# A fused attention and gated-FFN kernel: w_down loaded ahead of the x turns, the last FF-tile pair in 7 products, wo apart from down for token pair 0

## The chip, the cores and the metric

The kernel runs on one core of a Trainium2 chip. The metric is the device time of one execution, in microseconds (us). A core has a matrix engine (TensorE, PE in the profile), a vector engine (VectorE, DVE), a scalar engine (ScalarE, ACT), a general one (GpSimd, POOL) and SyncE (SP), which here only issues transfers. The engines run side by side and wait for each other by semaphores.

## The reference, cut to what matters

x has 2048 tokens of 512 features. It is normalized to xn. An attention branch A and a gated branch B both read xn, and their outputs are added to x:

```python
xn  = layernorm(x)                                       # 2048 x 512
q, k, v = split(xn @ wqkv)                               # 32 heads of 16
phi = lambda t: concat(softmax(t @ w_phi), softmax(-(t @ w_phi)))
kv  = sum_s phi(k)[s]^T v[s];  z = sum_s phi(k)[s]        # per head
o   = (phi(q) @ kv) / (phi(q) @ z + 1e-6)
A   = o @ wo
B   = ((xn @ w_gate) * (xn @ w_up)) @ w_down             # F = 1792
out = x + A + B
```

## The kernel before, in words

**Tiles.** The tokens are 16 tiles of 128 (t), 4 groups of 512 (sg), and 8 pairs of tiles (p) for the output. F is 14 FF tiles of 128 (ft); tiles ft and ft+7 form a pair, so there are 7 FF-tile pairs.

**Gate and up.** `U(ft, sg)` computes gate and up of one FF tile for one group: 4 + 4 matmuls of 512 columns, an eviction of gate by ACT (`ge`), and a multiplication on DVE that reads up from PSUM and writes `hT` (`h`). `BLOCK(kind, ft, ..)` does the same for an FF-tile pair and groups 1 and 2 at once, by a 2 x 2 scheme with 7 products in place of 8 (`b1` to `b7`, each 2 matmuls of 512 columns). It needs sums of weights (`WSUMS`, 4 on POOL for each block, `gw`, `uw`), sums of xn (`XSUMS`, 8 on DVE, `Xs`), and more evictions: seeds and copies on ACT (`sd`, `s7`, `s2`), adds on DVE (`a4`, `a5`). `NB` says how many pairs are done so. Group 3 is done later in halves of 256 tokens (`U2`, steps `gu`).

**Attention.** `K(t)`, `V(t)` and `KV(t)` build kv tile by tile; the features need a sum on DVE (`kr`), a reciprocal on ACT (`kc`) and two operations on POOL (`kq`, `kp`). `KVX` copies kv out. `Q(t)` makes the features of q (`qq`, `qp` on POOL) and turns them by a DMA (`qT`). `NUM(t)` multiplies by kv, divides, and turns the result by a DMA (`oT`).

**Down and wo.** Down is also a 2 x 2 scheme over each token pair, with 7 products `P1` to `P7` of 7 matmuls of 256 columns, sums of w_down (`TSUMS`, `Ts`, 16 on POOL) and of h (`SSUMS`, `S`, 4 on POOL for each pair). wo is joined in one of two ways. `CAT_STEPS(p)` puts wo into the same 7 products (2 more matmuls each, `P1o` to `P7o`), with 4 POOL sums of o for each pair (`SOSUMS`, `So`). `DOWN_STEPS(p)` adds wo in full to three products and one further group (`W22`), with no sums of o. `CAT` lists the pairs that take the first way.

**Normalization.** `LN(ts)` takes statistics on DVE (`st`, `ag`), scales on ACT into a ring of 4 slots (`nm`), and turns the tile by a DMA on SP (`xT`). So nm8 can be written only after xT4 has read its slot.

**Order.** Nothing runs in the order of the code. Each operation is recorded as a step with the regions that it reads and writes. A planner (`_plan`) then places the steps on each engine by costs, priorities and readiness, and the instructions are emitted in that order, with the semaphores that they need. `sc.chain` fixes the order of some steps: SP's loads and turns are one such chain. `PACE` and `SL` spread the block units over the K/V loop, and `UE`, `QP0`, `QP1` place group 3 and Q within the output pairs. Line 1449 holds w_down's place:

```python
sc.chain("x12 xT4 xT5 xT6 xT7 xT8 xT9 xT10 xT11 wd xT12 xT13 wT0 wo xT14 xT15")
```

Most instructions carry the line of a helper: L524 every matmul, L477 the evictions on ACT, L795 every sum (POOL, and DVE for XSUMS), L745 and L743 `kp`/`qp` and `kq`/`qq`, L825 and L876 the products h, L882 the adds of a block, L736 `kr`, L1203 the adds of down.

Of the kernel before, what the change touches and what calls it, by code (L numbers as in the profile page):

```python
# [57 lines left out]

class _Step:
    __slots__ = ("eng", "fn", "idx", "deps", "sig", "lane", "semval", "known", "waits", "is_out", "cost", "lat",  # L60
                 "prio", "seq", "start", "finish", "kind", "name", "nbytes", "ns", "win", "order", "lock", "reserve")

    def __init__(self, eng, fn, idx, lane):
        self.eng = eng
        self.fn = fn
        self.idx = idx
        self.deps = []
        self.sig = False
        self.lane = lane
        self.semval = None  # L70
        self.known = {}
        self.waits = []
        self.is_out = False
        self.cost = 100.0
        self.lat = 180.0
        self.prio = 0
        self.seq = 0
        self.start = 0.0
        self.finish = 0.0
        self.kind = ""  # L80
        self.name = ""
        self.nbytes = 0
        self.ns = ()
        self.win = 60.0
        self.order = []
        self.lock = False
        self.reserve = 0.0


# [111 lines left out]
def _plan(sc):  # L201
    nsteps = len(sc.steps)
    remaining = [0] * nsteps
    dependents = [[] for _ in range(nsteps)]
    for st in sc.steps:
        uniq = {id(d): d for d in st.deps}
        st.deps = list(uniq.values())
        remaining[st.idx] = len(st.deps)
        for d in st.deps:
            dependents[d.idx].append(st)  # L210
        for d in st.order:
            if id(d) not in uniq:
                remaining[st.idx] += 1
                dependents[d.idx].append(st)
    ready = {e: [] for e in sc.by_eng}
    ready_time = [0.0] * nsteps
    T0 = {PE: 800.0, ACT: 800.0, DVE: 800.0, POOL: 800.0, SP: 800.0}
    for st in sc.steps:
        ready_time[st.idx] = T0[st.eng]
        if remaining[st.idx] == 0:  # L220
            ready[st.eng].append(st)
    free_at = dict(T0)
    new_order = {e: [] for e in sc.by_eng}
    global_order = []
    dma_free = 0.0
    scheduled = 0
    while scheduled < nsteps:
        best = None
        for e in sc.by_eng:
            lst = ready[e]  # L230
            if not lst:
                continue
            fa = free_at[e]
            s0 = min(max(ready_time[st.idx], fa) for st in lst)
            cand = min((st for st in lst if max(ready_time[st.idx], fa) <= s0 + st.win),
                       key=lambda st: (st.prio, st.idx))
            s = max(ready_time[cand.idx], fa)
            if cand.lock:
                s = max(s, free_at[POOL])
            if best is None or s < best[0]:  # L240
                best = (s, cand)
        if best is None:
            raise RuntimeError("scheduling deadlock")
        start, st = best
        e = st.eng
        ready[e].remove(st)
        st.start = start
        if isinstance(st.lane, tuple):
            free_at[e] = start + st.cost
            if st.kind == "turn":  # L250
                d0 = max(start + st.cost + 410.0, dma_free)
                st.finish = d0 + st.nbytes / 182.0 + st.reserve
                dma_free = d0 + st.nbytes / 182.0 * 0.5
            else:
                d0 = max(start + st.cost + 1500.0, dma_free)
                dma_free = d0 + st.nbytes / 305.0
                st.finish = dma_free + (2500.0 if st.nbytes > 300000 else 0.0)
        else:
            free_at[e] = start + st.cost
            st.finish = free_at[e] + st.lat + st.reserve  # L260
            if st.lock:
                free_at[POOL] = max(free_at[POOL], free_at[e])
        st.seq = len(new_order[e])
        new_order[e].append(st)
        global_order.append(st)
        scheduled += 1
        for dep_st in dependents[st.idx]:
            remaining[dep_st.idx] -= 1
            in_order = st.eng == dep_st.eng and (st.eng == PE or not any(d is st for d in dep_st.deps))
            ready_time[dep_st.idx] = max(ready_time[dep_st.idx], free_at[e] if in_order else st.finish)  # L270
            if remaining[dep_st.idx] == 0:
                ready[dep_st.eng].append(dep_st)
    sc.by_eng = new_order
    sc.est_finish = max(st.finish for st in sc.steps)
    return global_order
# [76 lines left out]

XENG = DVE
LN12 = 6
FT = 7
QAT = [11, 12, 13, 14]
NB = 6
RS = 1
PA = -1
PD = -1  # L360
# [5 lines left out]
AB = {7: (2, 3)}  # L366
CO = {}
CH = "P6.7 P2.7 P5.7 P4.7 P3.7"
NX = 0
ZP = 0  # L370
WSE = POOL
# [2 lines left out]
NRA = ()  # L374
SD = ()
SPL = ((0, 7),)
UE = 1.6
QP0 = 1
QP1 = 2
QA = 4  # L380
PQ = -1
TRQ = 1500.0
TRO = 800.0
PS = -1
CAT = (0, 1, 2, 3, 4, 5, 6)
SOE = POOL
TOE = POOL
PLN = 0
RX = 1500.0
RG = 0.0  # L390
NSW = 2


SL = 11.5


def PACE(t, n):
# [3 lines left out]
def _build(nc, es, A_x, A_wqkv, A_w_phi, A_wo, B_w_gate, B_w_up, B_w_down, out):  # L401
# [68 lines left out]
    sc = _Sched(nc)  # L470
# [323 lines left out]
    def sums(eng, out_, a_, b_, op, name, prio=None):  # L794
        fn = lambda e: e.tensor_tensor(out=out_, in0=a_, in1=b_, op=op)  # L795
        n = out_.free_size()
        if eng == POOL:
            pool(fn, parts(a_) + parts(b_), parts(out_), 100.0 + 2.0 * n, name=name, prio=prio or 0)
        else:
            st = dve(fn, parts(a_) + parts(b_), parts(out_), cost=60.0 + 0.53 * n, name=name, prio=PX if prio is None else prio)  # L800
            st.lock = True
            st.reserve = RX if prio is None else 0.0

    hT_v = sbv("hT", 0, NF * 1536).bitcast(F16).rearrange("p (f s) -> p f s", f=NF)
# [596 lines left out]
    NA3 = len(units)  # L1401
    units += [(U2, ft, 1792) for ft in std]
    ui = [0]

    def weight(u):
        return 4 if u[0] is U2 or u[0] is U else 0 if u[0] is ZWSUMS else 1

    def nextU():
        if ui[0] < len(units):
            u = units[ui[0]]  # L1410
            if ui[0] == n0:
                ring_banks[0] = [2, 3, 4, 5]
            u[0](*u[1:])
            ui[0] += 1

# [8 lines left out]
    LN([8, 9], prio=PLN)  # L1424
    LN([10, 11], prio=PLN)
    load_wT(0)
    kvn = [0]

    def KVS(t, lag):
        while kvn[0] <= t - lag:  # L1430
            KV(kvn[0])
            kvn[0] += 1
    for t in range(NT):
# [10 lines left out]
        KVS(t, 3 if t < QAT[0] - 3 else 2)  # L1444
        if t == FT:
            FOLD(0)
    sc.dma(SP, wd_v, B_w_down.rearrange("(f p) j -> p f j", p=128), 1835008, writes=[wd_v], name="wd")
    load_sq(SP, wo_v, A_wo.rearrange("(q p) j -> p q j", p=128), 524288, "wo")
    sc.chain("x12 xT4 xT5 xT6 xT7 xT8 xT9 xT10 xT11 wd xT12 xT13 wT0 wo xT14 xT15")
    TSUMS()  # L1450
    V(NT - 1)
    KVS(NT, 2)
    SSUMS(0)
    assert ui[0] >= NA
    load_x(SP, 4, 4, name="rx")
    load_x(SP, 8, 4, name="rx")
    down = CAT_STEPS(0) if 0 in CAT else DOWN_STEPS(0)
    nextU()
    KVS(NT, 1)
    KVX()  # L1460
    ring_banks[0] = [0, 1, 2, 3]
    rp[0] = 0
    nextU()
    if 0 not in CAT:
        down[0]()
        down[1]()
    NUM(0)
    nextU()
    if 0 not in CAT:
        SSUMS(1)  # L1470
    nextU()
    NUM(1)
    TOSUMS(TOE)
    if 0 in CAT:
# [6 lines left out]
        cum.append(cum[-1] + weight(u))  # L1481
    u0 = ui[0]
    NP = NT // 2
    for p in range(NP):
        def some(fr):
            k = cum[-1] * min(1.0, (p + fr) / (NP - UE))
            while ui[0] < len(units) and cum[ui[0] - u0] + weight(units[ui[0]]) / 2 <= k:
                nextU()
        if p == ZP and NX:
            ZXSUMS()  # L1490
            for b_ in blocks[:3]:
                ZWSUMS(*b_)
        a, b = 2 * p + 2, 2 * p + QA
        if p == 2:
            load_x(SP, 12, 4, name="rx", slot=0)
        def Qs(pos):
            for k, at in ((0, QP0), (1, QP1)):
                if at == pos and b + k < NT:
                    Q(b + k)
        if p in AB:  # L1500
            ring_banks[0] = [0, 1]
        if p > 0:
            down = CAT_STEPS(p) if p in CAT else DOWN_STEPS(p)
            Qs(0)
            down[0]()
            some(0.1)
            Qs(1)
            down[1]()
        some(0.2)
        if a < NT:  # L1510
            NUM(a)
        if p == 0:
            Qs(0)
            Qs(1)
        Qs(2)
        down[2]()
        some(0.4)
        Qs(3)
        down[3]()
        if 2 <= p + 1 < NP and p + 1 not in SLATE:  # L1520
# [12 lines left out]
        some(1.0)  # L1533
        if p + 1 in SLATE:
            SSUMS(p + 1)
        down[7]()
# [46 lines left out]
```

The softmax here doesn't subtract the row's maximum and nothing guards it: scores larger than these inputs give would overflow.

## Time and profile before

| | |
|---|---|
| time, median of 4 runs | 211.43 us (210.92 to 211.73) |
| time of the profiled execution | 210.92 us |
| its span, first to last instruction | 209.1 us |
| granted TensorE clock | 1.0 |
| busy: PE, POOL, DVE, ACT | 204.9, 174.1, 158.5, 113.7 us |
| loads of x, 512 KB: issue to landing (median) | 5.3 us |
| load of w_down, 1792 KB: issue to landing | 7.8 us |

Times in rows of the profile are us from the start of the span. Busy time of PE is modelled at its ends, so a full PE is not PE at its peak. "PEld" is the load of weights into PE ahead of matmuls. In rows of groups the numbers behind the bar are the busy time in us, the mean of one in ns, and the idle time of the engine before them with what ended it. In rows of a time line they are the start and the length in us.

### The profile page before, as it was taken

The page shows a single profiled execution, that of the slowest core. Times are in us where ns is not written, and L with a number is a line of the kernel's source. Part 1 is how long each engine was busy: PE and PEld are TensorE (multiplying, and loading weights), DVE is VectorE, ACT ScalarE, POOL GpSimd, SP SyncE. Part 2 cuts the span into 40 slices and gives each one's busy share as a digit, 9 for nine tenths or more (in the row PEclk, how much of TensorE's full clock was granted, in tenths as well). Part 3 has the DMA queues.
Part 4 walks back from the last instruction along what each step waited for, and adds up shares of the span by engine and source line. Part 5 has one row for each costly group of instructions (what it writes and reads, how often), then busy time and mean ns, then how long its engine had stood idle before and what let it go on. Part 6 is the DMA issues. An engine that isn't in the chain of part 4 may idle for free.

```text
span 209.1 us, 4281 instructions
## 1 busy us (share of the span) xinstructions
PE 204.9 (98%) x1616; PEld 135.7 (65%) x1616; DVE 158.5 (76%) x305; ACT 113.7 (54%) x293; POOL 174.1 (83%) x223
## 2 busy tenths in 40 slices
PE   8999999999999999999999999999999999999995
PEld 3875444444454444444446797888879888789884
DVE  4857799998966797989988766848659486584753
ACT  4756999698796959697822633315244151431000
POOL 4071698439999999999999999999999999997640
PEclk9999999999999999999999999999999999999999
DMA  5999724965100000223621217455351655435121
GB/s 173 330 277 371 211 61 97 342 115 144 37 16 0 3 0 0 50 52 53 193 60 28 50 25 138 91 128 105 70 131 25 141 38 115 91 75 129 27 75 50
DMA packets 50244, 21.52 MB, mean 103 GB/s; under 512 B 37424, under 2 KB 50224, under 8 KB 50224
## 3 DMA queue, kind: packets, MB, share of 16 engines
q1 hardware_dynamic: 49552, 20.93, 41.3%
q10 hardware_dynamic: 672, 0.33, 0.6%
q8 instruction: 12, 0.20, 0.4%
q14 instruction: 8, 0.07, 0.1%
HBM read 10.24 MB, written 2.10 MB: 59 GB/s over the span
## 4 chain that ended last, share of the span: by engine, by line
PE 81%; ACT 7%; POOL 4%; DVE 3%; DMA 3%; issue 1%; DVEq 0%
PE ps L524 79%; ACT arena L477 7%; DMA arena<-arena 3%; PE ps L1345 2%; POOL arena L795 2%; POOL arena L745 1%; DVE arena L641 1%; DVE arena L795 1%; DVE arena L736 1%; DVE arena L825 0%; POOL arena L743 0%; ACT ps L477 0%; DVE arena L643 0%; DVE arena L1203 0%; POOL arena L650 0%
## 5 line engine op out<-in xcount | busy, mean ns | idle before, releaser
L524 PE MATMUL ps<-arena 128*128 128x256 bf16 (+5 forms) x1606 | 200.7, 287 | 0.9 <-ACT ps L477 0.3
L524 PEld LDWEIGHTS ps<-arena 128*128 128x128 bf16 (+1 forms) x1606 | 134.4, 98 | 67.8 <-ACT arena L477 2.0
L795 POOL TENSOR_TENSOR arena<-arena 128x256 f16<-128x256 bf16 (+3 forms) x128 | 129.3, 1032 | 7.4 <-DMA arena<-arena 3.4
L477 ACT ACTIVATE arena<-ps 128x512 bf16<-128x512 f32 (+3 forms) x168 | 83.1, 533 | 65.2 <-PE ps L524 62.1
L736 DVE TENSOR_REDUCE arena<-arena 128x64 f32<-128x1024 bf16 x32 | 38.7, 1211 | 0.9 <-ACT arena L477 0.9
L1203 DVE TENSOR_TENSOR arena<-ps,arena 128x256 bf16<-128x256 f32 (+1 forms) x56 | 23.1, 421 | 17.9 <-PE ps L524 16.3
L477 ACT ACTIVATE arena<-arena 128x64 f32<-128x64 f32 (+4 forms) x96 | 28.4, 314 | 13.7 <-DVE arena L736 10.4
L745 POOL TENSOR_TENSOR arena<-arena 128x512 bf16<-128x512 bf16 x32 | 33.7, 1056 | 0.2
L1069 DVE TENSOR_TENSOR arena<-ps,arena 128x256 f16<-128x256 f32 x30 | 12.6, 421 | 11.1 <-ACT arena L477 11.0
L876 DVE TENSOR_TENSOR arena<-ps,arena 128x512 f16<-128x512 f32 x24 | 16.1, 684 | 1.0 <-PE ps L524 0.8
L825 DVE TENSOR_TENSOR arena<-ps,arena 128x512 f16<-128x512 f32 x14 | 9.5, 687 | 4.1 <-PE ps L524 2.5
L770 DVE TENSOR_TENSOR arena<-ps,arena 128x512 bf16<-128x512 f32 x16 | 10.9, 684 | 2.1 <-ACT arena L477 1.5
L641 DVE BATCH_NORM_STATS2 arena<-arena 128x6 f32<-128x512 bf16 x16 | 10.5, 675 | 1.9 <-DMA arena<-in_A_x_dram 1.9
L882 DVE TENSOR_TENSOR ps<-ps,arena 128x512 f32<-128x512 f32 x12 | 8.2, 696 | 4.3 <-PE ps L524 3.0
L1137 DVE TENSOR_TENSOR arena<-ps,arena 128x512 bf16<-128x512 f32 x16 | 11.0, 686 | 0.3
L743 POOL TENSOR_TENSOR arena<-arena 128x32 f32<-128x32 f32 x32 | 8.2, 260 | 3.2 <-ACT arena L477 3.2
L650 POOL TENSOR_SCALAR arena<-arena 128x1 f32<-128x1 f32 x12 | 3.3, 288 | 6.9 <-ACT arena L477 6.9
L623 POOL TENSOR_TENSOR arena<-arena 128x128 bf16<-128x128 bf16 x4 | 1.6, 425 | 8.5 <-DMA arena<-in_A_w_phi_dram 8.5
L882 DVE TENSOR_TENSOR arena<-ps,arena 128x512 bf16<-128x512 f32 x12 | 8.0, 680 | 0.0
L477 ACT ACTIVATE ps<-ps 128x512 f32<-128x512 f32 x12 | 7.2, 600 | 0.0
L1133 DVE RECIPROCAL arena<-arena 128x32 f32<-128x32 f32 x16 | 5.6, 352 | 0.5
L1345 PE MATMUL ps<-const-bfloat16-1.0 128*128 128x512 bf16 x10 | 4.4, 623 | 0.8 <-PEq L1568 0.8
(22 smaller groups left out, 26.0 us busy)
## 6 DMA issues: line engine op xcount, KB each, us to landing
arena<-in_A_x_dram SPq DMA_DIRECT2D x6, 512.0 KB, 5.3
arena<-in_B_w_down_dram SPq DMA_DIRECT2D x1, 1792.0 KB, 7.8
out_dram<-arena SPq DMA_DIRECT2D x14, 128.0 KB, 2.0
arena<-in_B_w_gate_dram SPq DMA_DIRECT2D x1, 768.0 KB, 7.2
arena<-in_B_w_up_dram SPq DMA_DIRECT2D x1, 768.0 KB, 8.8
arena<-arena SPq DMA_TRANSPOSE x44, 2.5
arena<-in_B_w_gate_dram SPq DMA_DIRECT2D x2, 256.0 KB, 4.2
arena<-in_B_w_gate_dram SPq DMA_DIRECT2D x1, 512.0 KB, 5.9
```

The costliest lines, as they stand in the source:

```text
L477: return e.activation(out=out_ap, in_=in_ap, func=func, scale=scale, **kw)
L524: ins = e.matmul(o, lhsT=l, rhs=r, start=s, stop=p, skip_group_check=True)
L641: dve(lambda e, t=t: e.bn_stats(stats_v[:, t, :], x_tile(t)), [x_tile(t)], [stats_v[:, t, :]], cost=600.0, name=f"st{t}", win=win, prio=prio)
L736: dve(lambda e, ei=ei, so=so: e.tensor_reduce(out=so, in_=ei.rearrange("p (h f) -> p h f", f=16), axis=AX.X, op=ALU.add), [ei], [so], cost ...
L745: pool(lambda e: e.tensor_tensor(out=ev[:, :, 1, :], in0=ev[:, :, 1, :], in1=ratio[:, :, None].to_broadcast([128, H, 16]), op=ALU.mult), [ ...
L770: dve(lambda e: e.tensor_tensor(out=o1, in0=src, in1=rp_[:, :, :, None].to_broadcast([128, 8, 4, 16]), op=ALU.mult), [src, rs_v[:, t % 4, ...
L795: fn = lambda e: e.tensor_tensor(out=out_, in0=a_, in1=b_, op=op)
L876: dve(lambda e: e.tensor_tensor(out=h, in0=src, in1=g, op=ALU.mult), [src, g], [h], name=f"h{ft}.{sg}", prio=PD)
L882: dve(lambda e: e.tensor_tensor(out=o, in0=src, in1=sn, op=ALU.add), [src, sn], [o], name=name, prio=PD)
L1069: dve(lambda e: e.tensor_tensor(out=h, in0=bank(b, 256 - GLO, 256), in1=g, op=ALU.mult), [bank(b, 256 - GLO, 256), g], [h], name=f"h{ft}.{ ...
L1137: dve(lambda e: e.tensor_tensor(out=ov, in0=src, in1=wv4[:, :, :, None].to_broadcast([128, 8, 4, 16]), op=ALU.mult), [src, w], [o], cost=6 ...
L1203: dve(lambda e: e.tensor_tensor(out=out_, in0=in_ps, in1=in_sb, op=ALU.add), [in_ps, in_sb], [out_], cost=328.0, name=f"{name}.{p}")
```

## The change

Three things and the settings that go with them. w_down's load stands after x12 in SP's chain, ahead of all turns of x (`WDP`), and its step is recorded earlier. `NB` is 7, so gate and up of all seven pairs take the 7 products in groups 1 and 2, and the four units `U` of tiles 6 and 13 there are gone. `CAT` begins at 1: pair 0 takes `DOWN_STEPS`. Group 3's units are not issued ahead of the pair loop any more (`nextT`, `p_done`). `FT`, `UE`, `QP1`, `SL` and `RX` have new values. The planner also gets a rule for DVE sums that are marked `sync`, which makes a POOL step wait for them.

```diff
-                 "prio", "seq", "start", "finish", "kind", "name", "nbytes", "ns", "win", "order", "lock", "reserve")
+                 "prio", "seq", "start", "finish", "kind", "name", "nbytes", "ns", "win", "order", "lock", "sync", "slip", "reserve")
...
             if st.lock:
                 free_at[POOL] = max(free_at[POOL], free_at[e])
+                if st.sync:
+                    port.append([st, st.slip, st.slip > 1])
+            elif e == POOL:
+                for q in port:
+                    if q[2] and last_pool is not None and last_pool not in st.deps:
+                        st.deps.append(last_pool)
+                    q[2] = False
+                    q[1] -= 1
+                    if q[1] <= 0 and q[0] not in st.deps:
+                        st.deps.append(q[0])
+                port = [q for q in port if q[1] > 0]
...
-FT = 7
+FT = 8
-NB = 6
+NB = 7
+WDP = 'x12'
+TT = None
...
-UE = 1.6
+UE = 1.8
-QP1 = 2
+QP1 = 3
...
-CAT = (0, 1, 2, 3, 4, 5, 6)
+CAT = (1,2,3,4,5,6)
...
-RX = 1500.0
+RX = 0.0
...
-SL = 11.5
+SL = 11.85
...
             st.lock = True
+            st.sync = prio is not None
+            st.slip = SLIP
             st.reserve = RX if prio is None else 0.0
...
     load_wT(0)
+    sc.dma(SP, wd_v, B_w_down.rearrange("(f p) j -> p f j", p=128), 1835008, writes=[wd_v], name="wd")
...
-    sc.dma(SP, wd_v, B_w_down.rearrange("(f p) j -> p f j", p=128), 1835008, writes=[wd_v], name="wd")
+        if t == TT:
+            TSUMS()
     load_sq(SP, wo_v, A_wo.rearrange("(q p) j -> p q j", p=128), 524288, "wo")
-    sc.chain("x12 xT4 xT5 xT6 xT7 xT8 xT9 xT10 xT11 wd xT12 xT13 wT0 wo xT14 xT15")
-    TSUMS()
+    order = "x12 xT4 xT5 xT6 xT7 xT8 xT9 xT10 xT11 xT12 xT13 wT0 wo xT14 xT15".split()
+    order.insert(order.index(WDP) + 1, "wd")
+    sc.chain(" ".join(order))
+    if TT is None:
+        TSUMS()
     V(NT - 1)
+
+    def nextT():
+        if ui[0] < NA2:
+            nextU()
...
     down = CAT_STEPS(0) if 0 in CAT else DOWN_STEPS(0)
-    nextU()
+    nextT()
```

More of the change, by code (lines that the diff above doesn't have):

```diff
@@ L86, in __init__ @@
         self.lock = False
+        self.sync = False
+        self.slip = 1
         self.reserve = 0.0
@@ L226, in _plan @@
     scheduled = 0
+    port = []
+    last_pool = None
     while scheduled < nsteps:
@@ L262, in _plan @@
                 free_at[POOL] = max(free_at[POOL], free_at[e])
+                if st.sync:
[9 more added lines that the diff above has]
+                port = [q for q in port if q[1] > 0]
+            if e == POOL:
+                last_pool = st
         st.seq = len(new_order[e])
@@ L354 @@
 LN12 = 6
-FT = 7
-QAT = [11, 12, 13, 14]
-NB = 6
+FT = 8
+QAT = [11,12,13,14]
+NB = 7
+WDP = 'x12'
+TT = None
 RS = 1
@@ L368 @@
 CH = "P6.7 P2.7 P5.7 P4.7 P3.7"
+SLIP = 2
+SYN = (".0", ".1")
 NX = 0
@@ L1403, in _build @@
     ui = [0]
+    p_done = [False]
     def weight(u):
@@ L1412, in nextU @@
                 ring_banks[0] = [2, 3, 4, 5]
+            assert ui[0] < NA2 or p_done[0]
             u[0](*u[1:])
@@ L1462, in _build @@
     rp[0] = 0
-    nextU()
+    nextT()
     if 0 not in CAT:
@@ L1467, in _build @@
     NUM(0)
-    nextU()
+    nextT()
     if 0 not in CAT:
         SSUMS(1)
-    nextU()
+    nextT()
     NUM(1)
@@ L1483, in _build @@
     NP = NT // 2
+    p_done[0] = True
     for p in range(NP):
```

## The prediction

> **What bounds the kernel now.** I read the page's first part, then busy time by stage, then the matmuls of each stage by form, then the time lines of the queues around the moved load.
>
> ```profile
> PE 204.9 (98%) x1616; PEld 135.7 (65%) x1616; DVE 158.5 (76%) x305; ACT 113.7 (54%) x293; POOL 174.1 (83%) x223
> ...
> 40.00:57.00 17.00, 16.35 (x96) 7.26 (x95) 16.02 (x26) 15.20 (x39) 12.94 (x20) 1.00 0.52 126
> 57.00:107.00 50.00, 50.00 (x319) 24.24 (x320) 42.94 (x59) 39.09 (x99) 50.00 (x68) 1.00 0.20 44
> 107.00:206.00 99.00, 99.00 (x937) 82.24 (x934) 68.20 (x150) 30.34 (x79) 90.48 (x86) 1.00 0.38 79
> ```
>
> The columns of a stage row are PE, PEld, DVE, ACT and POOL busy, then granted clock, DMA share and GB/s. PE is full nearly everywhere, and POOL is full from 57 to 107. A full PE row need not mean work, since matmul ends are modelled. So I price a column in two stages whose shapes differ:
>
> ```profile
> L524 PE MATMUL ps<-arena 128*128 128x512 bf16 x145 | 35.7, 379 | 0.3 <-ACT ps L477 0.3
> L524 PE MATMUL ps<-arena 128*128 128x512 f16 x70 | 19.7, 379 | 0.0
> L524 PE MATMUL ps<-arena 128*128 128x68 bf16 x88 | 4.4, 194 | 0.0
> L524 PE MATMUL ps<-arena 128*128 128x128 bf16 x16 | 1.4, 219 | 0.0
> ...
> L524 PE MATMUL ps<-arena 128*128 128x256 bf16 x442 | 53.1, 273 | 0.0
> L524 PE MATMUL ps<-arena 128*128 128x256 f16 x280 | 34.2, 273 | 0.0
> L524 PE MATMUL ps<-arena 128*128 128x512 bf16 x72 | 18.0, 379 | 0.0
> L524 PE MATMUL ps<-arena 128*128 128x68 bf16 x139 | 7.4, 194 | 0.0
> ```
>
> The first four rows are 57 to 107: 215 x 512 + 88 x 68 + 16 x 128 = 118,112 columns in 50.0 us, 0.423 ns each. The last four are 107 to 205.6: 231,148 columns in 98.6 us, 0.427 ns. The price is the same, so PE does not stall in either; it is the bound by its column count. Only 40 to 57 differs: 72 x 512 + 24 x 68 = 38,496 columns at 0.423 are 16.3 us of 17.0, so 0.7 us of stall can be won back there. POOL, full, is a second engine with little room: what it delivers late, PE pays for one to one.
>
> **The change part by part.** The sum is made against the profiled execution (210.92 us, span 209.1). That is the lowest of the four times; the median is 211.43, so I apply the difference to the median.
>
> *Products for pair 6.* Before, gate and up of FF tiles 6 and 13 for groups 1 and 2 are 4 units of 8 matmuls of 512 columns: 32. After, two blocks of 7 products of 2 matmuls: 28. PE: -4 x 512 columns = -2,048. POOL: 8 sums of 128x256 at 0.67 us = +5.4 us. ACT: 8 evictions for 4, +4 x 0.60 = 2.4 us. DVE: 4 more adds on PSUM, +4 x 0.69 = 2.7 us. In 57 to 107 ACT is idle for 10.9 us and DVE for 7.1, so by sum both hold it; those two cost nothing while that idle time lasts, and up to 2.7 us without it.
>
> *Pair 0 of down without wo.* The joined form has 7 x (7+2) = 63 matmuls of 256 columns. The plain form has 49, then 12 for wo in P4, P2, P3 and 4 for W22: 65. PE: +512 columns. POOL loses the 4 sums So.0, -4 x 0.67 = -2.7 us. DVE has one 0.42 us post more, where it is idle for 30.8 of 99 us: nothing.
>
> PE in sum: -1,536 columns x 0.424 ns = **-0.65 us**. No cover hides this.
>
> *w_down moved.* The queue of SP before:
>
> ```profile
> 14.08 1.87 SPq L175 DMA_DIRECT2D arena<-in_A_x_dram  x2
> 22.71 12.42 SPq L174 DMA_TRANSPOSE arena<-arena  x8
> 35.18 0.58 SPq L175 DMA_DIRECT2D arena<-in_B_w_down_dram  x1
> ```
>
> The new place is after x12, at 15.95, where SP has nothing to issue until 22.71. The 0.58 us of issue is hidden. Behind it on the queue are xT4 to xT13, wT0, wo, xT14, xT15, which keep their order. The data is not hidden. x8 and x12 need about 9.2 us from issue to landing (the median of the three 512 KB x loads in 10 to 50), for a 128 KB x alone it is 2.1: transfers stand in line. The Trainium skill ("DMA: Bandwidth & Descriptors", section "Queues, rings and completion order") says that each DMA engine consumes the descriptors of a queue in ring order. That rule speaks against this change: the 1.84 MB stand between x12 and xT4. By the row alone, xT4 lands 2.5 us after its issue, at 25.2, and nothing moves. By the rule, x12's data ends near 23.2, w_down at the 375 GB/s of that stage takes 4.9 us to 28.1, and xT4 lands near 30, an estimate, +4.8 us. I take the rule: x12's row looks the same way.
>
> Who waits for xT4? The ring of normalized tiles has four slots, so nm8 (ACT) waits for it, then xT8 to xT11, then the sums Xs on DVE, then the first product b7g.0.
>
> ```profile
> 29.18 1.74 ACT L477 ACTIVATE arena<-arena 128x512 bf16<-128x512 bf16 x4
> ...
> 36.43 1.84 DVE L795 TENSOR_TENSOR arena<-arena 128x512 f16<-128x512 bf16 x4 [0.22 <-DMA arena<-arena]
> ```
>
> nm8 is the first of those at 29.18. In the new order it stands behind both ke2, kc1 and vz1: k2 ends at 29.5, and 2 x 0.595 plus three of 0.24 less overlaps put nm8 at 31.0. xT4, at 30, is hidden by 1.0 us there. nm8 is then 1.8 us later, so xT11 lands at 38.2 instead of 36.4, and the four sums that b7g.0 needs end at 39.7 to 40.1. b7g.0 stands at the same column as before, which was 39.95. So 0 to 0.2 us of stall, and up to 0.5 at b4g.0, moved to third place, which needs Xs3.1 and s7g.0.
>
> Two more Xs at 39.33 took 0.74 us with POOL idle, 0.37 each; two at 41.79 took 1.32 with POOL at work, 0.66 each. The skill ("SBUF — State Buffer", section "Who interferes with whom") says that a DVE instruction with two SBUF inputs contends with a GpSimd instruction that reads SBUF, and the loser blocks for all of it. With Ts (1.16 us) now on POOL beside the Xs, the rule would put up to 1.2 us on each of the last four, b4g.0 some 2 us late; the row puts 0.3 on each. I take the row, because POOL waits for kq3 and b7g.0 just then (after Ts0.2 and kp2, near 38.6), and Ts0.4 comes only behind kp3. Against that stand the 0.7 us of stall of this stage now, whose waits (a4g.0 and sdu.1) fall in another order. Bounds for the stage: -0.7 if all is won, +2 by the port rule; I take **-0.3**.
>
> *TSUMS on POOL.* They wait for w_down. Before, POOL in this stretch:
>
> ```profile
> 35.59 0.27 POOL L743 TENSOR_TENSOR arena<-arena 128x32 f32<-128x32 f32 x1 [0.74 <-ACT arena L477]
> 37.78 0.77 POOL L650 TENSOR_SCALAR arena<-arena 128x1 f32<-128x1 f32 x2 [0.79 <-ACT arena L477]
> 40.63 0.27 POOL L743 TENSOR_TENSOR arena<-arena 128x32 f32<-128x32 f32 x1 [2.07 <-ACT arena L477]
> 46.19 1.88 POOL L795 TENSOR_TENSOR arena<-arena 128x896 f16<-128x896 f16 x1 [3.35 <-DMA arena<-arena]
> ```
>
> 6.95 us idle from 35 to 46. In the new order Ts0.0 follows uw4.1 (near 34.8), with five Ts before kq4: 4 x 1.12 + 0.63 = 5.1 us of it filled. With three weight sums that come forward and S1.0 that leaves, I count **5.8 us** filled.
>
> What POOL must do before kp15, on which the last kv product waits, grows by 8 weight sums (8 x 0.625 back to back) and four S sums placed ahead of it (4 x 1.84): 12.4 us. PE's columns before kv15 grow from 244,704 to 260,576, 6.7 us. kp15 ended at 107.2 (POOL's time line: L745 at 105.16, 2.07 long, two of them), kv15 began at 108.6, just ahead of kvx at 109.1: margin 1.4. New margin: 1.4 + 6.7 + 5.8 - 12.4 = **1.5 us**. The same at P7o.1, which waits for So3.1: 2.8 + 3.8 + 5.8 - 10.5 = 1.9. So POOL is early enough, without much to spare; I take **+0.2** for waits I cannot place (bounds 0 and 2).
>
> *Where four gate/up units left.* Around kvx and n0, PE now has P1.0, q4, P7.0, gu1, gu0 ahead of kv15 and P6.0, q5 behind it: 1.83 us until n0, before it was 1.93 with 0.8 spare. No stall. On SP rx4 and rx8 now follow qT3 and wait for the last block of pair 6 (h13.2, near 111), with oT0 behind, whose data (no0) comes near 118; oT1 and oT2 stand behind qT4 and qT5 (qp4 near 118, qp5 near 123.5), their data near 121 and 125. Each reaches its product with over 1 us to spare: nothing, and up to 1 us if qp5 were 2 us late, which is POOL again. The fields sync and slip add no dependency: only a DVE sum with a given priority sets them, and XSUMS gives none; RX only lets the planner place the Xs users earlier.
>
> Sum: -0.65 - 0.3 + 0.2 = **-0.75 us**, so 211.43 - 0.75, about **210.7 us**.
>
> **The rivals.** *Columns win, waits stay as they are or shrink* (0.58): -0.65 to -1.6, 209.8 to 210.8. For it: one column price in two stages and margins over 1 us.
>
> *New waits eat the gain* (0.16): 0.1 to 1.2 us at b7g.0, b4g.0 or an eviction in 57 to 107, where DVE is busy for 86%: 210.8 to 212.0. For it: Xs has 0.2 us to spare.
>
> *POOL becomes the bound* (0.26), slower: POOL reaches kp15 after PE reaches kv15. It decides from the moment that less than 4.3 us of the idle time is filled. If w_down lands 3 us later than estimated, or a Ts waits for a slot behind kq3 or gw3.2, which wait for ACT and PE, only 3 us are filled: 1.3 us late. With 1 us more it is 2.3. Less the 0.65: +0.65 to +1.65, 212.1 to 213.1. Against it: 6.95 us stand idle there.
>
> **How the numbers follow.** About 0.3% (0.6 us) is what a measurement of this kernel can tell from no change. Faster than that: the first case nearly whole, 0.56. Within: the second and the edges of the others, 0.18. Slower: 0.26. The range reaches from 209.6 (all of the stall won and 0.4 of run spread) to 212.5 (POOL 1.7 us late); what lies outside is some 2 in 10. The likeliest case alone is 209.8 to 210.8.
>
> **What would show it.** Right: PE again one price per column from 57 on, the 40 to 57 stage no more than 0.7 us over its columns, POOL busy from about 41 on instead of 46, w_down landing near 29 with the first xT at 30. Wrong: PE waiting for POOL L745 or L795 near 114 to 136 (POOL the bound), or DVE L795 beginning after 39.5 with PEld waiting for it (w_down in the way of xT), or new waits of PEld for DVE L882 in 57 to 107.

## The result, and the profile after

The changed kernel takes 210.57 us (median of 42 runs, 209.89 to 211.50) against 211.27 us (63 runs of before, 210.48 to 212.46). The ratio is 0.9969, 95% interval 0.9959 to 0.9978: 0.70 us faster. The prediction on record was 210.7 us, 0.75 us faster. The profiled execution has a span of 208.4 us (before 209.1) and a granted clock of 1.0 throughout.

The line numbers have moved: L545 is now the matmul (L524 before), L498 the evictions on ACT (L477), L816 every sum (L795), L766 and L764 `kp` and `kq` (L745, L743), L848 and L899 the products h, L791 `vs`, L757 `kr`. First the busy time on the page of the changed kernel, then its busy time by stage (columns as before: PE, PEld, DVE, ACT, POOL, granted clock, DMA share, GB/s).

```profile
PE 204.5 (98%) x1614; PEld 135.5 (65%) x1614; DVE 158.2 (76%) x310; ACT 116.2 (56%) x297; POOL 177.6 (85%) x227
```

```profile
40.00:57.00 17.00, 16.94 (x113) 7.97 (x111) 14.89 (x26) 14.16 (x37) 16.67 (x25) 1.00 0.36 86
57.00:107.00 50.00, 50.00 (x293) 23.64 (x290) 43.38 (x61) 40.33 (x101) 50.00 (x68) 1.00 0.11 19
107.00:205.00 98.00, 98.00 (x943) 81.84 (x942) 69.31 (x155) 32.34 (x85) 88.53 (x84) 1.00 0.43 93
```

PE is as full as it was. POOL has 3.5 us more work, and from 40 to 57 it is busy for 16.67 us instead of 12.94: that is where the idle time before S1.0 went. The matmuls by form, 57 to 107 and then 107 to 204.9, price a column again:

```profile
L545 PE MATMUL ps<-arena 128*128 128x512 bf16 x141 | 35.2, 379 | 0.0
L545 PE MATMUL ps<-arena 128*128 128x512 f16 x80 | 21.8, 379 | 0.0
L545 PE MATMUL ps<-arena 128*128 128x68 bf16 x56 | 2.9, 194 | 0.0
L545 PE MATMUL ps<-arena 128*128 128x128 bf16 x16 | 1.4, 219 | 0.0
...
L545 PE MATMUL ps<-arena 128*128 128x256 bf16 x452 | 55.1, 272 | 0.0
L545 PE MATMUL ps<-arena 128*128 128x256 f16 x272 | 33.8, 272 | 0.0
L545 PE MATMUL ps<-arena 128*128 128x512 bf16 x60 | 15.4, 379 | 0.0
L545 PE MATMUL ps<-arena 128*128 128x68 bf16 x152 | 7.9, 194 | 0.0
L545 PE MATMUL ps<-arena 128*128 128x512 f16 x6 | 1.8, 378 | 0.0
```

The first four rows are 221 x 512 + 56 x 68 + 16 x 128 = 119,008 columns in 50.0 us, 0.420 ns each; the other five are 229,472 columns in 97.9 us, 0.427 ns each. Before it was 0.423 and 0.427. The edges of a stage cut through matmuls, one of 512 columns being 0.2 us, so within that the price of a column did not move, and 1,536 columns fewer are 0.65 us.

The rest, PE's time from its first to its last matmul less 0.423 ns for each column, is 5.30 us before and 5.26 us after. The small difference hides shifts. From 20 to 40 there is 0.46 us more, from 40 to 60 there is 0.63 us less, from 100 to 130 there is 0.06 more, and in the first 10 us there is 0.13 more. The last is no effect of the change: up to there the order of the steps is the same in all 14 kernels that were traced, and this part of the rest goes from 2.6 to 3.7 us among them, one traced execution each. The last matmul ends 0.69 us earlier.

The early part is told by the time lines of SP, ACT, POOL and DVE. SP's time line after:

```profile
16.25 2.27 SPq L177 DMA_DIRECT2D arena<-in_B_w_down_dram  x1
22.85 14.30 SPq L176 DMA_TRANSPOSE arena<-arena  x8
```

The issue of w_down takes 2.27 us instead of 0.58. The page of the profile gives 14.0 us from issue to landing (before 7.8), so it lands at 30.25. Behind it, the issue of xT4 alone is held for 3.08 us in the trace, against 1.19 for an undisturbed one, and xT4 lands at 30.77, xT6 at 33.23, xT7 at 34.43, xT11 at 38.44. ACT's time line shows who waits, nm8 and nm9 first, then nm10, then nm11:

```profile
31.21 1.50 ACT L498 ACTIVATE arena<-arena 128x512 bf16<-128x512 bf16 x2
33.25 0.81 ACT L498 ACTIVATE arena<-arena 128x512 bf16<-128x512 bf16 x1 [0.54 <-DMA arena<-arena]
34.46 0.96 ACT L498 ACTIVATE arena<-arena 128x512 bf16<-128x512 bf16 x2 [0.39 <-DMA arena<-arena]
35.32 0.57 ACT L498 ACTIVATE arena<-ps 128x512 bf16<-128x512 f32 x1
```

The last line is the eviction ge11.0. It stands behind nm11, and on PE g13.0 waits for it: 0.45 us at 35.95, the new stall of the stage from 20 to 40. POOL's time line next:

```profile
40.33 1.58 POOL L764 TENSOR_TENSOR arena<-arena 128x32 f32<-128x32 f32 x1 [1.44 <-ACT arena L498]
41.87 0.66 POOL L816 TENSOR_TENSOR arena<-arena 128x256 f16<-128x256 bf16 x1
```

The first line is kq3. It takes 1.58 us instead of 0.27 (before, at 40.63). It ends at 41.91, and DVE's eight sums Xs run back to back from 39.02 to 41.78, each in 0.42 us:

```profile
39.02 2.76 DVE L816 TENSOR_TENSOR arena<-arena 128x512 f16<-128x512 bf16 x8
```

The product kv15 waits for POOL's kp15. That one is the first line here and ends at 114.93; kv15 starts at 115.24, so 0.31 us are to spare:

```profile
113.88 1.06 POOL L766 TENSOR_TENSOR arena<-arena 128x512 bf16<-128x512 bf16 x1
114.89 1.89 POOL L816 TENSOR_TENSOR arena<-arena 128x896 f16<-128x896 f16 x1
```

### The profile page after: what moved, and what is told of

It is laid out like the page before. It is cut to its first block, busy times and chain, and to the rows that moved or that the text cites. A ratio compares the mean times of both kernels' runs of the same rounds, so it can differ in the third digit from the quotient of the medians.

```text
span 208.4 us, 4286 instructions
## 1 busy us (share of the span) xinstructions
PE 204.5 (98%) x1614; PEld 135.5 (65%) x1614; DVE 158.2 (76%) x310; ACT 116.2 (56%) x297; POOL 177.6 (85%) x227
## 4 chain that ended last, share of the span: by engine, by line
PE 91%; ACT 3%; DMA 3%; DVE 2%; issue 1%; DVEq 0%
PE ps L545 89%; ACT arena L498 3%; DMA arena<-arena 3%; PE ps L1368 2%; DVE arena L662 1%; DVE arena L848 0%; DVE arena L664 0%; DVE arena L1226 0%; DVEq L366 0%; DVE arena L1289 0%
## 5 line engine op out<-in xcount | busy, mean ns | idle before, releaser
L545 PE MATMUL ps<-arena 128*128 128x256 bf16 (+5 forms) x1604 | 200.3, 287 | 0.6 <-ACT arena L498 0.3
L545 PEld LDWEIGHTS ps<-arena 128*128 128x128 bf16 (+1 forms) x1604 | 134.2, 98 | 67.3 <-ACT arena L498 3.0
L816 POOL TENSOR_TENSOR arena<-arena 128x256 f16<-128x256 bf16 (+3 forms) x132 | 132.2, 1026 | 4.2 <-DMA arena<-arena 2.0
L498 ACT ACTIVATE arena<-ps 128x512 bf16<-128x512 f32 (+3 forms) x170 | 84.0, 535 | 61.1 <-PE ps L545 59.2
L757 DVE TENSOR_REDUCE arena<-arena 128x64 f32<-128x1024 bf16 x32 | 38.7, 1211 | 2.0 <-ACT arena L498 1.9
L498 ACT ACTIVATE arena<-arena 128x32 f32<-128x32 f32 (+4 forms) x96 | 28.6, 317 | 13.2 <-DVE arena L757 10.0
L766 POOL TENSOR_TENSOR arena<-arena 128x512 bf16<-128x512 bf16 x32 | 33.9, 1061 | 0.1
L899 DVE TENSOR_TENSOR arena<-ps,arena 128x512 f16<-128x512 f32 x28 | 18.5, 685 | 3.9 <-PE ps L545 3.8
L791 DVE TENSOR_TENSOR arena<-ps,arena 128x512 bf16<-128x512 f32 x16 | 10.9, 684 | 2.1 <-PE ps L545 2.1
L764 POOL TENSOR_TENSOR arena<-arena 128x32 f32<-128x32 f32 x32 | 9.7, 306 | 2.4 <-ACT arena L498 2.1
L905 DVE TENSOR_TENSOR ps<-ps,arena 128x512 f32<-128x512 f32 x14 | 9.5, 693 | 2.6 <-ACT arena L498 2.4
L1160 DVE TENSOR_TENSOR arena<-ps,arena 128x512 bf16<-128x512 f32 x16 | 11.0, 685 | 0.2
L848 DVE TENSOR_TENSOR arena<-ps,arena 128x512 f16<-128x512 f32 x10 | 6.8, 687 | 4.2 <-ACT arena L498 2.3
L905 DVE TENSOR_TENSOR arena<-ps,arena 128x512 bf16<-128x512 f32 x14 | 9.4, 682 | 0.3 <-ACT arena L498 0.3
L498 ACT ACTIVATE ps<-ps 128x512 f32<-128x512 f32 x14 | 8.4, 601 | 0.1
```

The lines of the kernel that those rows point to most:

```text
L498: return e.activation(out=out_ap, in_=in_ap, func=func, scale=scale, **kw)
L545: ins = e.matmul(o, lhsT=l, rhs=r, start=s, stop=p, skip_group_check=True)
L757: dve(lambda e, ei=ei, so=so: e.tensor_reduce(out=so, in_=ei.rearrange("p (h f) -> p h f", f=16), axis=AX.X, op=ALU.add), [ei], [so], cost ...
L766: pool(lambda e: e.tensor_tensor(out=ev[:, :, 1, :], in0=ev[:, :, 1, :], in1=ratio[:, :, None].to_broadcast([128, H, 16]), op=ALU.mult), [ ...
L791: dve(lambda e: e.tensor_tensor(out=o1, in0=src, in1=rp_[:, :, :, None].to_broadcast([128, 8, 4, 16]), op=ALU.mult), [src, rs_v[:, t % 4, ...
L899: dve(lambda e: e.tensor_tensor(out=h, in0=src, in1=g, op=ALU.mult), [src, g], [h], name=f"h{ft}.{sg}", prio=PD)
```

## The experiments

Two theories were held against each other. One: the gain is the columns, POOL's full row is near its limit, and the move of w_down pays by feeding POOL early. The other: each of the three named parts gains or costs something on its own, and the sum of these is the result. A first set does one part alone in the kernel before, a second set undoes one part or doses one cost in the kernel after. Ratios are to the kernel before, from the same chip; "after" is the changed kernel, its own ratio is 0.9969. In every kernel in which a setting or a load differs, the planner places the steps anew; where the order was held, the text says so.

### w_down alone

This and the next two kernels have the code of after with the settings of before, apart from the line shown. With `WDP = 'xT11'` that code places every step as in the kernel before.

```diff
-WDP = 'xT11'
+WDP = 'x12'
```

> The kernel before, with w_down's load moved ahead of the x turns and nothing else (NB, CAT and all settings as before; the planner orders anew). PE's columns are those of before. Theory C (PE's columns set the time, waits are a small rest): no change but the stalls of 30 to 57 us; the changed kernel showed +0.45 us there at g13.0 and -0.6 later, so -0.3 to +0.4 us. Rival M (the move of the load is what gains, by giving POOL room early): -0.5 us or more.

Ratio 1.0035 (1.0017 to 1.0053): 0.75 us slower, with the same 473,600 columns. Both expectations missed. The old stalls of 40 to 57 are gone, but three new ones stand in the trace: 0.68 us at g13.0, 0.34 at k5 and 0.83 at v4. The last of these waits for vs3 on DVE, whose time line says why vs3 is late:

```profile
39.16 1.42 DVE L816 TENSOR_TENSOR arena<-arena 128x512 f16<-128x512 bf16 x4
40.50 0.68 DVE L848 TENSOR_TENSOR arena<-ps,arena 128x512 f16<-128x512 f32 x1
41.10 0.68 DVE L791 TENSOR_TENSOR arena<-ps,arena 128x512 bf16<-128x512 f32 x1
41.70 1.87 DVE L816 TENSOR_TENSOR arena<-arena 128x512 f16<-128x512 bf16 x2
```

Four Xs take 1.42 us with POOL idle; two take 1.87 us once POOL has begun the weight sums. One of these, Xs2.1, takes 1.37 us instead of 0.42: it ends 0.28 us after the POOL sum Ts0.4, which began ahead of it. vs3 stands behind it and behind kr4. So Ts now runs beside Xs, and DVE is the one that is held. The hold alone is not the loss, though: the eight Xs take 4.44 us one by one, and in the kernel before 4.29 (undisturbed, as in after, 3.36). There vs3 stood ahead of the sum that was held. The planner's new order and the hold act together; no run took them apart.

### The seventh pair alone

```diff
-NB = 6
+NB = 7
```

> The kernel before with NB = 7 and nothing else: 2,048 PE columns fewer, w_down still behind the x turns, pair 0 still joined with wo. Theory C: -2,048 x 0.424 ns = -0.87 us, if POOL holds: its work before kp15 grows by 6.9 us, PE's before kv15 by 7.6, so the margin of 1.4 becomes 2.1 us. Rival M (POOL cannot take 8 more weight sums without the early start of TSUMS): less than 0.3 us gained, or slower, with PE waiting for POOL between 60 and 135 us.

Ratio 1.0248 (1.0212 to 1.0284): 5.2 us slower, though PE has 2,048 columns fewer. None of the lost time stands at the added products (98.6 to 112); some 0.6 us lies between 60 and 100, nearly all the rest behind 120. The stage from 120 to 140 shows it:

```profile
120.00:140.00 20.00, 16.26 (x154) 12.33 (x153) 13.77 (x33) 4.63 (x14) 20.00 (x21) 0.91 0.58 102
```

POOL is busy for all of it and PE is not. PE's waits, by name in the trace: P7o.0 1.71 us for So3.0, n3 1.09 for no2 on DVE, P6o.0 1.01 for So2.0. The granted clock of 0.91 is a mean:

```profile
125.00:131.00 6.00, 3.43 (x43) 2.44 (x41) 4.74 (x11) 0.78 (x4) 6.00 (x8) 1.00 0.44 90
131.50:134.90 3.40, 3.08 (x15) 2.21 (x16) 1.38 (x3) 0.00 (x0) 3.40 (x4) 0.50 1.27 137
```

In the second row the clock is 0.50, and P4.0 and P5.0, each 7 matmuls of 256 columns, take 1.70 and 1.52 us instead of 0.93: 1.4 us that are no wait. The mean clock was 0.992 in five of the six executions; the one at 1.000 took 214.93 us, still 3.7 above before. So POOL's waits are the larger part, and the slower clock that came with them is the rest.

The expectation of the gain had looked at kv15 as the first place where POOL could be late. That margin held (2.78 us); the one at P7o.0, 0.42 us in the kernel before, did not.

### Pair 0 without wo alone

```diff
-CAT = (0, 1, 2, 3, 4, 5, 6)
+CAT = (1,2,3,4,5,6)
```

> The kernel before with pair 0 of down taken out of the joined form and nothing else: 512 PE columns more, four POOL sums fewer. Theory C: +0.22 us. Rival M: POOL gains 2.7 us of room, but nothing waited for it, so also about +0.2; a gain here would mean that the So sums of pair 0 (0.42 and 0.53 us ahead of their products before) hold PE up in some executions.

Ratio 1.0033 (1.0012 to 1.0054): +0.7 us with an interval of 0.45 to either side, where 512 columns are 0.22. In the traced execution 0.5 us of the excess lies in the first 10 us, which this edit does not touch and where the executions scatter. From there on PE's rest is that of before, 2.56 us in both, so the trace shows the columns and no new wait. Nothing here gains.

### The three parts with the settings of before

```diff
-FT = 8
+FT = 7
-UE = 1.8
+UE = 1.6
-QP1 = 3
+QP1 = 2
-RX = 0.0
+RX = 1500.0
-SL = 11.85
+SL = 11.5
```

> The kernel before with the three named parts together (w_down ahead of the turns, NB = 7, pair 0 without wo) and the old settings (FT, UE, QP1, RX, SL). Columns as changed. If the three parts together are the gain, since the moved load and the dropped sums of pair 0 make the room on POOL that pair 6 takes: within 0.4 us of the changed kernel, -0.3 to -0.7 against before. If the settings carry it (the pace at which the seventh pair's products are handed to the planner, RX for the order of the Xs users): +1 us or more against the changed kernel, with waits between 100 and 140 us.

Ratio 1.0094 (1.0071 to 1.0116), with the 472,064 columns of after: 1.25% above after, 2.6 us. The stalls at g13.0 (0.59), k5 (0.34) and v4 (0.83) are those of w_down alone, and 0.57 us at P1o.1 and 0.15 at kv14 come in. The size is what was expected if the settings carry the gain, the place only in part: of the 2.6 us, 0.85 lie between 100 and 150, and 1.4 between 20 and 100. The settings are part of the change's effect, not trimming: with the old ones the three parts lose. Which of the five does it was not separated.

### After, with w_down where it was

```diff
-WDP = 'x12'
+WDP = 'xT11'
```

> The changed kernel with w_down's load back behind xT11, all else changed. Columns as changed. Theory C: 0.65 us under before, or more by the 0.45 us of g13.0, which had waited for turns behind w_down: -0.65 to -1.1 us. Rival M (without early TSUMS POOL is late): kp15 would end near 87.8 + 28.2 = 116.0 where kv15 is due at 115.2, So3.1 at 135.3 where its product is due at 134.9: +0.8 us against the changed kernel, so about no change against before.

Ratio 0.9994 (0.9980 to 1.0008), so 0.25% or 0.5 us above after; the intervals of the two do not meet. The g13.0 stall is gone, k5 has 0.34 us, and P1o.1 has 0.57 in place of 0.12. The size is the one that the rival gave, the place is not: kp15 ends at 114.97 and So3.1 at 134.13, as early as in after. P1o.1 waits for a DMA turn:

```profile
130.39 5.81 PE L545 MATMUL ps<-arena 128*128 128x256 bf16 x61 [0.38 <-DMA arena<-arena]
```

It is oT2, which stands behind qT5 on SP's queue, and qT5 waits for qp5 on POOL. The planner has put two sums of 1.88 us, S1.1 and S2.1, behind kp15 here and ahead of it in after, and qp5 ends at 125.16 instead of 124.41. So POOL's room does show, through qp5 and a turn. It is not the whole: 0.65 us more than in after lie between 60 and 100, and their cause was not followed. In the kernel after, the early load gains; in the kernel before, it loses.

### After, with wo in pair 0's products

```diff
-CAT = (1,2,3,4,5,6)
+CAT = (0,1,2,3,4,5,6)
```

> The changed kernel with pair 0 joined with wo again: 512 columns fewer, four POOL sums So.0 more. Theory C: -0.22 us against the changed kernel, -0.9 against before. Rival P (that part of the change was needed since POOL has 0.3 to 0.8 us to spare from 110 to 137): 2.7 us of sums between 110 and 125 us make So3.1 and qp4 later, PE waits 0.5 to 2 us: equal to before or slower.

Ratio 1.0130 (1.0084 to 1.0175): 3.4 us above after, with 512 columns fewer. PE's waits for POOL's sums from 110 to 140, in this kernel:

```profile
PE ps L545 <- POOL arena L816: 1.8, 2, 1.1
```

The two are P7o.0 (So3.0) and P6o.0 (So2.0), the same places as with the seventh pair alone. Four sums So of 0.67 us each, 2.7 us of POOL, bring POOL's waits back. Not all of the 3.4 us are POOL's: the new order also has 1.26 us at g13.0 (after 0.45), and the clock has a share. Of the five executions that the ratio rests on, the two with a mean clock of 1.000 took 212.99 and 213.46 us, the three at 0.991 to 0.992 took 214.20 to 215.25. Against the former it is 2.4 to 2.9 us.

### After, with 2,048 columns more on PE, same order

```diff
-            for (o, l, r, s, p) in items:
+            for (o, l, r, s, p) in items * (2 if name == 'gu5.1536' else 1):
```

> The changed kernel, order untouched, with one gate/up unit of group 3 (gu5 of tokens 1536) computed twice: 8 matmuls of 256 columns more, 2,048 columns. Theory C: +2,048 x 0.424 = +0.87 us against the changed kernel, so about +0.2 us against before. Rival (PE is modelled full but has room near there): under +0.3 us against the changed kernel.

Ratio 0.9994 (0.9971 to 1.0017), 0.25% above after, with an uncertainty as large; the profiled span is 209.2, 0.8 us longer than after's. 2,048 columns at 0.425 ns are 0.87. The profile agrees with the price, the ratio alone only allows it.

### After, with 1.8 us more on POOL ahead of kp15, same order

```diff
+TWICE = ('S3.1',)
...
+            if name in TWICE:
+                e.tensor_tensor(out=sbv('dummy', 0, 861).bitcast(F16).rearrange('p (k j) -> p k j', k=7), in0=a_[:, :, 0:123], in1=b_[:, :, 0:123], op=op)
```

> The changed kernel, order untouched, with one POOL sum of 128x896 (S3.1, ahead of kp15) done nearly twice, the extra one of 128x861 into a scratch region: +1.8 us of POOL work where the trace shows kp15 only 0.31 us ahead of kv15. If POOL is next to being the bound (a thin margin): 1.8 - 0.3 = 1.5 us late at kv15, +1.5 us against the changed kernel, so +0.8 against before, with PE waiting for POOL near 115 us. If the margin is wider (a late kp15 is covered): under +0.4 us.

Ratio 1.0046 (1.0026 to 1.0067), 1.6 us above after. In POOL's time line, first the added sum, last kp15; below it PE's time line, where kv15 waits for kp15:

```profile
112.19 1.84 POOL L820 TENSOR_TENSOR arena<-arena 128x861 f16<-128x861 f16 x1
...
115.81 1.07 POOL L768 TENSOR_TENSOR arena<-arena 128x512 bf16<-128x512 bf16 x1
```

```profile
116.93 2.25 PE L547 MATMUL ps<-arena 128*128 128x68 bf16 x25 [1.51 <-POOL arena L768]
```

1.8 us put on POOL are 1.6 us on the end, and the stage from 100 to 130, where kv15 stands, has as much (PE's rest there is 1.93 us, in after 0.35). The margin of after, 0.31 us, is about what is missing.

### After, with w_down behind xT5

```diff
-WDP = 'x12'
+WDP = 'xT5'
```

> The changed kernel with w_down behind xT5 instead of ahead of xT4. Columns as changed. If the 0.45 us at g13.0 comes from xT6 and xT7 standing behind w_down with SP's issue held up (3.08 us for xT4's issue against 1.2), then xT4 and xT5 land near 26 and the later ones still wait; the stall may stay or move to b7g.0: -0.4 to +0.6 us against the changed kernel. A version better than it only if PE loses nothing between 30 and 57 us.

Ratio 1.0043 (1.0020 to 1.0067). The g13.0 stall does not come back as such; 0.98 us at k5 (for h13.0), 0.59 at b1g.0 and 0.66 at P6o.2 stand in its place. It is 1.6 us above after, outside what was expected.

### After, with w_down in two halves

```diff
-    sc.dma(SP, wd_v, B_w_down.rearrange("(f p) j -> p f j", p=128), 1835008, writes=[wd_v], name="wd")
+    wd_s = B_w_down.rearrange("(f p) j -> p f j", p=128)
+    sc.dma(SP, wd_v[:, 0:7], wd_s[:, 0:7], 917504, writes=[wd_v[:, 0:7]], name="wd")
+    sc.dma(SP, wd_v[:, 7:14], wd_s[:, 7:14], 917504, writes=[wd_v[:, 7:14]], name="wd2")
...
+    order.insert(order.index("xT12") + 1, "wd2")
```

> The changed kernel with w_down's load in two halves: rows 0 to 6 of its 14 FF tiles ahead of xT4, which is all that the first quarter of TSUMS reads, rows 7 to 13 behind xT12. Columns as changed. Theory Q (w_down's 1.84 MB ahead of the turns make nm10 and nm11 wait for xT6 and xT7, and so g13.0, 0.45 us in the changed kernel's trace, more in others; POOL needs only the first half early): xT4 lands near 28, nm8 is back at 29.2, no stall at g13.0, POOL as early as before: -0.4 to -0.8 us against the changed kernel, -1.1 to -1.5 against before. Rival (the early part of the kernel is bound by DVE and ACT whatever the turns do): the stall moves to b7g.0 or k5, within 0.2 us of the changed kernel.

Ratio 1.0021 (0.9999 to 1.0044), 1.1 us above after. The queue does what the halves were meant for: xT4 lands at 28.07 instead of 30.77, its issue takes 1.21 us instead of 3.08, xT6 and xT7 land at 29.03 and 29.46, and g13.0 does not wait. But k5 waits 1.30 us for h13.0 on DVE, more than was won. DVE:

```profile
36.66 4.17 DVE L816 TENSOR_TENSOR arena<-arena 128x512 f16<-128x512 bf16 x8 [0.17 <-DMA arena<-arena]
40.75 1.21 DVE L757 TENSOR_REDUCE arena<-arena 128x64 f32<-128x1024 bf16 x1
41.88 0.68 DVE L848 TENSOR_TENSOR arena<-ps,arena 128x512 f16<-128x512 f32 x1
```

Eight Xs take 4.17 us, where after's eight take 2.76. In the trace Xs2.1 takes 1.27 us and ends 0.28 us after kp2 on POOL, and Xs0.0 takes 0.88 beside Ts0.2.

### The halves, with h13.0 and kr3 changed over on DVE, all else in its order

```diff
     global_order = _plan(sc)
+    step = {st.name: st for st in global_order}
+    a, b = step["kr3"], step["h13.0"]
...
+    line = sc.by_eng[a.eng]
+    line.remove(a)
+    line.insert(line.index(b) + 1, a)
...
```

> The halves of w_down (second half behind xT12) left one wait of 1.30 us at k5 for h13.0, which stands on DVE behind eight Xs and kr3. Here only two neighbours on DVE change places in that kernel: h13.0 goes ahead of kr3, all else stays. Theory D (the one wait is the whole loss of the halves): h13.0 ends near 41.4, when k5 can begin at 41.54, the wait is 0.1 or less, the span falls from 210.1 to 208.9, ratio to before 0.9955 to 0.997, level with the change as it was made or below it by no more than the g13.0 wait of 0.45. Rival (the stall moves): kr3 is 0.7 us later, kc3 and vs3 behind it too, v4 waits for vs3 and kv3 for kp3, and 0.3 to 0.9 us come back between 44 and 50: ratio 0.9985 to 1.001.

Ratio 0.9995 (0.9969 to 1.0020), inside the rival's range and outside theory D's; the two intervals, of this and of the halves, overlap. In the profile k5's wait falls from 1.30 to 0.16, and 0.90 us appear at v4. It waits for vs3, and vs3 for kc3, which stands behind the later kr3: the chain that the rival named. Busy time from 36.6 to 46, in before, then after, then this kernel:

```profile
36.60:46.00 9.40, 9.40 (x65) 4.49 (x63) 9.40 (x17) 7.62 (x21) 3.29 (x6) 1.00 0.79 230
```

```profile
36.60:46.00 9.40, 9.34 (x64) 4.38 (x63) 8.88 (x20) 7.64 (x20) 7.85 (x10) 1.00 0.14 28
```

```profile
36.60:46.00 9.40, 8.67 (x54) 3.72 (x53) 9.39 (x17) 7.49 (x21) 6.71 (x11) 1.00 0.25 67
```

DVE is the third number behind the comma. It is full in before and here, and in the halves and in w_down alone as well (9.34 and 9.40); after has 0.52 us to spare, with 20 instructions done instead of 16 to 19. A full row of DVE is not all work: the eight Xs take 3.36 us one by one when nothing holds them, as in after, and 4.29, 4.68, 4.44 and 4.53 in before, the halves, w_down alone and here. So 0.9 to 1.3 us of DVE's busy time in these 9 us is time held beside POOL; after pays it on POOL instead, in kq3. With so little room on DVE, changing two of its steps over changed who waits more than how long.

### After, with w_down on ACT's queue

```diff
-    sc.dma(SP, wd_v, B_w_down.rearrange("(f p) j -> p f j", p=128), 1835008, writes=[wd_v], name="wd")
+    sc.dma(ACT, wd_v, B_w_down.rearrange("(f p) j -> p f j", p=128), 1835008, writes=[wd_v], name="wd")
```

> The changed kernel with w_down issued by ACT, on ACT's queue, at about the time of x12, everything on SP's queue without it. If the turns wait for w_down only since they stand behind it in SP's queue, they land as before (xT4 near 25.5, SP's issue of it 1.2 us instead of 3.1) and g13.0 does not stall; ACT pays one issue. If instead the 16 DMA engines are shared whatever the queue, the turns are slowed by about half of the 5 us for as long as w_down flows. First case -0.4, second 0 to +0.5 us against the changed kernel.

Ratio 1.0319 (1.0293 to 1.0345). Two things are mixed here. The load, issued at 25.64 and 10.2 us on its way by the page of the profile, stretches the turns that are under way on SP's queue: xT5 lands at 30.42, xT6 at 35.83, xT7 at 36.42, 5.5 to 9.6 us after their issue, where an undisturbed turn takes 2.4. That says that another queue gives no separate way. But the planner also put nm8 at 39.62 on ACT, though xT4 had landed at 26.27, so xT8 is issued at 40.44 and Xs begins at 48.20. That late order, with waits of 1.99, 1.30 and 0.93 us on PE, carries most of the time, and the granted clock was 0.50 from 49.9 to 53.2. The ratio says nothing on the queue alone.

## Why the prediction was right

**The sum.** -0.65 us by columns was the main term and stands: the price of a column is the same in both stages, and PE's rest moved by only -0.04 us. The total of -0.75 came out as -0.70. The terms behind the columns, though, are right in sum rather than one by one: the +0.2 for waits on POOL did not come, since PE has no wait for POOL in after. What fills its place is 0.13 us in the first 10 us, which is scatter, and 0.06 from 100 to 130. That the total fits to 0.05 us is luck.

**The stage from 40 to 57.** I took -0.3 for the early part, from bounds of -0.7 and +2. It is -0.63 from 40 to 60 and +0.46 from 20 to 40, -0.17 together. The waits at b7u.0 (0.47) and b2u.1 (0.52) are gone, as I thought possible. I put the price of the late turns at b7g.0 and b4g.0 (0.24 us in the end); I did not put one on nm10 and nm11, behind which an eviction and then g13.0 wait. I had checked nm8 against its turn on ACT, and not what stands behind nm11 there.

**The load.** The ring rule of the skill ("DMA: Bandwidth & Descriptors", section "Queues, rings and completion order") held: xT4 lands at 30.77, where the rule gave 30 and the row of before 25.2; nm8 at 31.21 against 31.0, xT11 at 38.44 against 38.2. Two steps within are wrong and cancel. I had x12's data end near 23.2; it landed at 24.65 before and at 25.10 after (23.25 is x8). And I had left 2 us from w_down's landing to that of xT4; it was 0.5, as behind the half load, which lands at 27.55 and xT4 at 28.07. That half the bytes bring xT4 2.7 us forward agrees with the rule. It is not the only reading: on ACT's queue the same load stretched turns as well, so no run separates the order within a queue from the sharing of the DMA engines.

**The port.** Here I took the row (0.3 us on each Xs) against the rule ("SBUF — State Buffer", section "Who interferes with whom"). The section calls the shared pair of ports an exclusive lock. It says that the loser is blocked for a whole instruction only of DVE's two-port modes; of DVE instructions with two SBUF inputs, as Xs is, it says that they contend with GpSimd's reads. In after, neither the row nor the rule came true on DVE: the Xs took 0.42 us each, and POOL's kq3 was held for 1.3 us. I had weighed only one direction. The kernels with w_down alone and with the halves show a block of that kind, single Xs of 1.37 and 1.27 us that end 0.28 us after a POOL sum. So does before: the pair of 1.32 us that I had spread over two is one of 0.52 and one of 0.88, and the second ends 0.28 us after gw3.2. So the rule as I had put it describes the single instruction, and my mean over two had hidden it. That the sums Xs in after escaped it fits with POOL waiting for kc3 as they began, so that kq3 came second; no run separates this from another cause.

**POOL.** I gave kv15 a margin of 1.5 us and P7o.1 one of 1.9, and +0.2 for unplaced waits. In the trace kp15 ends at 114.93 and kv15 starts at 115.24, 0.31 us; P7o.1 has 0.77. Term by term for kv15: POOL's work before kp15 grew by 13.1 us where I had 12.4, 5.4 us of its idle time were filled where I had 5.8, and kv15 came 6.6 us later where I had 6.7. That is the 1.2 us which the margin lost; at P7o.1 the first two make the 1.1. The largest single item in the work is kq3, held for 1.3 us; nb12 and gw3.2, which were held in before, took 0.5 less. POOL has no idle time from kq3 to kp15, so what it lost there carried through. So the direction was right, and the rival in which POOL becomes the bound stood closer than I wrote: the run with 1.8 us more on POOL pays 1.6 of them.

**Pair 0.** I costed the plain form as 512 columns and noted 2.7 us less on POOL without giving it a worth. It is a condition of the whole: with wo left in pair 0, the kernel after is 3.4 us slower (2.4 to 2.9 at full clock), with 1.8 to 2.2 us of waits for So2.0 and So3.0 in the profile. My POOL count had these sums out already, so the forecast was not wrong by it, but the text named the cost of the step and not what it buys.

**What would have misled.** A sum of the parts measured alone would be +0.75, +5.2 and +0.7 us. Together they are +2.0 with the old settings and -0.70 with the new ones. The load feeds POOL, the plain pair 0 relieves it, the seventh pair spends both, and the settings place the steps so that it fits.

## What to carry to other kernels

Where one engine is full by its work and a second has margins of tenths, a change that shifts work from the first to the second is to be judged together with what makes room on the second; each part alone can lose. Compute the margin of the second engine at every place where the first takes its results (here kv15, P7o.0, P6o.0, P7o.1), since the first one that fails sets the price. And when a stall moves instead of going, look for an engine that is full over just that stretch, and for how much of its busy time is work and how much is time held by another engine.

## What the runs showed of the hardware

Operations of DVE and POOL that both read and write SBUF held each other up singly and in both directions: kq3 took 1.58 us instead of 0.27 while DVE ran Xs, and an Xs took 1.27 or 1.37 us instead of 0.42 while POOL ran a sum. The price depends on who comes second, so a load moved by some microseconds changed which engine paid.

A DMA's issue on SP is not a fixed cost. w_down's took 2.27 us behind the x loads instead of 0.58, and the turn behind it 3.08 us instead of 1.19; behind half the bytes the turn took 1.21, though the issue of that half took 2.25.

The granted clock fell to 0.50 for 3.4 us after PE had waited much. With the seventh pair alone that was from 131.50 on, with w_down on ACT's queue from 49.88. In the 3.4 us just before, PE had 1.07 and 0.95 us of work, and no single wait was longer than 1.5 and 2.0 us. With wo in pair 0's products, 1.76 us of work in 3.4 (127.6 to 131.0) were followed by a clock of 1.00. Not every execution of one kernel had it: of six of the seventh pair alone, one kept a mean of 1.000 and was 1.2 to 2.3 us shorter than the others. So a wait of PE can cost more than its own length. No run here tells where the limit lies.
